# Products of ones on TensorE ahead of the first transposes of k, q and P

## The chip, the cores and the metric

The kernel runs on one core of one Trainium2 chip. The metric is the time of one execution in microseconds (us). Three executions of the kernel before took 773.11, 776.22 and 777.68 us, a median of 776.22 us. One more execution was profiled; all durations below come from that one.

## The reference

Two layers, one after the other. Attention with pooled queries: q, k and v are (4, 8, 1152, 64) in float32; pairs of query rows are averaged, so that 576 query rows per head meet 1152 keys. Then a feed-forward layer over the 2304 tokens of 512 features, with a squared ReLU between two matrices of 512 x 2048 and 2048 x 512.

```
q_pool = q.reshape(B, H, S // 2, 2, D).mean(axis=3)
scores = (1 / sqrt(D)) * q_pool @ k.T
attn   = exp(scores - max(scores)); attn = attn / (sum(attn) + 1e-09)
x      = (attn @ v), heads laid side by side: (2304, 512)
out    = relu(x @ w_in) ** 2 @ w_out
```

## The kernel before

**Tiling.** Two heads of one batch are a pair; there are 16 pairs. A pair's 2 x 576 query rows are cut into 9 chunks of 128 rows, so there are 144 chunks, each with a score tile of 128 x 1152. For a chunk TensorE forms the scores (S), VectorE finds the row maximum (MX), ScalarE takes the exponential and its row sum (EX), giving P. P is then transposed, and multiplied by v (PV). Once a block of 256 tokens has all its heads it goes through the feed-forward layer: H (first matrix, line 1033), the square, O (second matrix, line 1082). There are nine such blocks.

**Precision.** In most pairs operands are split into a high and a low 16-bit part, and transposed by DMA. The first pair takes another way (`full_s`): its k and q are transposed on TensorE in float32, as products with the identity, into PSUM banks "ba", and copied from there: KX (k, three groups of 6 matmuls, line 423) with its copies KC (lines 415 and 417), QS (the sum of query pairs on VectorE, line 400), QY (q, two groups, line 436) with its copies QC. The scores of this pair are float32 too (line 653, two chunks at a time). The chunks of the first four pairs (`full_v`) transpose their P on TensorE in float32: TP (line 750, three groups of 3 matmuls) with copies TC (lines 760 and 762). A float32 matmul has two records in the trace, one matmul in the program.

**Beside it.** While the first chunks run, the weights are loaded in 16 pieces of 1 MB (line 1136) and converted: 1144, 1150 and 1163 are ScalarE's steps of a piece, 1153, 1169 and 1178 VectorE's (some of them go to GpSimd). Line 466 is a product of the raw k, q or v with itself (GR), which gives that pair's scale; line 470 takes its maximum (GM).

**What sets the order.** A table, `ORDER`, lists every step with its engine and its buffer. Each engine runs its steps strictly in that order, and waits by semaphores for what it reads and for buffers that others must give back. There are two banks "ba" until the last chunk is done; the six banks "bt" come later. The DMAs are issued from SP's queue, in order as well: the load of the second pair's k (line 369) waits until KX has read the first pair's, the load of the second q (line 377) until QY has.

The functions `kx`, `qy` and `tp4` are emitted for KX, QY and TP; `bank(o, ...)` gives the bank that the table chose for the step. `ones` is a column of 128 ones in bfloat16, written by the first instruction of VectorE (line 1326).

Of the kernel before, what the change touches and what calls it, by code (L numbers as in the profile page):

```python
# [16 lines left out]
AX = mybir.AxisListType  # L17
PSUM = bass.MemoryType.PSUM

CFG = {'SPLIT': 0, 'TURN': [], 'TURNB': [], 'WDP': ((1, 0), (1, 1), (1, 2), (1, 3)), 'WSP': 0.4394, 'WOF': 23.2581, 'MSP': 10.7319, 'FV': (0, 1, 2, 3), 'PART': 1, 'QXD': (1, 2, 3, 4), 'MSC': (0, 1, 2, 3, 4, 5, 6, 7, 8, 9, 10, 11, 12, 13, 14, 15), 'FS': (0,), 'NSG': (12, 13, 14, 15)}  # L20


def cfg(k, d):
    return CFG.get(k, d)

# [73 lines left out]
class Plan:  # L99
# [7 lines left out]
    def add(self, name, engs, deps, emit, at, take=None, give=None, after=()):  # L107

        self.at[name] = len(self.ops)
        self.ops.append(  # L110
            dict(name=name, engs=engs, deps=[d for d in deps if d], emit=emit, take=take, give=give, after=after)
        )
# [30 lines left out]
def kernel(  # L143
# [12 lines left out]
    nc = tc.nc  # L156
# [27 lines left out]
    ones = c_p.tile([128, 1], BF16, name="ones")  # L184
# [56 lines left out]
    def bank(o, *shape):  # L241
        r, x = plan.slot[o["name"]]
        t = banks[r][x]
        if not shape:
            return t
        return t[:, : shape[0] * shape[1]].rearrange("p (a b) -> p a b", a=shape[0])

    def buf(*key):
        r, x = plan.slot[key]
        return bufs[r][x]  # L250
# [12 lines left out]
    def alt(kind, **engs):  # L263
        on = cfg("alt", {}).get(kind, ALT.get(kind, ""))
        return {e: c for i, (e, c) in enumerate(engs.items()) if i == 0 or e[0] in on}
# [25 lines left out]
    def kT(n):  # L291
        s = preps[n]["slot"]
        return kTs[s] if s is not None else buf("kT", n).rearrange("p (a b) -> p a b", b=128)

    def qT(n):
        s = preps[n]["slot"]
        return qTs[s] if s is not None else buf("qT", n).rearrange("p (l c m) -> p l c m", l=2, c=9)

    def k4(n):
        return kT(n).rearrange("p a b -> p (a b)").bitcast(F32).rearrange("p (c k) -> p c k", c=9)  # L300

    def q4(t):
        return t.rearrange("p l c m -> p (l c m)").bitcast(F32).rearrange("p (c m) -> p c m", m=64)
# [13 lines left out]
    def pslot(vi, j, full):  # L317
        t = PT.rearrange("p a s b -> p (a s b)")
        if full:
            t = t.bitcast(F32)  # L320
        a = pcol(vi, j)
        return t.rearrange("p (a x) -> p a x", x=896)[:, :, a : a + 128]
# [24 lines left out]
    def prep(n):  # L347
# [11 lines left out]
        def rk():  # L359
            return raw("k", n).rearrange("p (h c d) -> p h c d", h=2, c=9)  # L360
# [4 lines left out]
        def rq():  # L365
            return raw("q", n).rearrange("p (c r d) -> p c r d", c=9, r=2)
# [35 lines left out]
        def k2():  # L402
            return buf("k2", n).rearrange("p (h c l d) -> p h c l d", h=2, c=9, l=2)
# [5 lines left out]
        if n in full_s:  # L409
            assert not keep  # L410
            kt4, qt4 = k4(n), q4(qT(n))

            def move(o, out, x):
                if o["eng"] == "ACT":
                    nc.scalar.activation(out, x, AF.Copy)
                else:
                    nc.vector.tensor_copy(out, x)

            def kx(o, x):
                tl["kx", n, x] = t = bank(o, 3, 128)  # L420
                for y in range(3):
                    for h in range(2):
                        nc.tensor.matmul(
                            t[h * 64 : h * 64 + 64, y], lhsT=rk()[:, h, 3 * x + y, :], rhs=ident,
                            start=True, stop=True, skip_group_check=True,
                        )

            def kc(o, x):
                move(o, kt4[:, 3 * x : 3 * x + 3], tl.pop(("kx", n, x)))

            def qy(o, z):
                tl["qy", n, z] = t = bank(o, 5, 64)
                for y in range(5 - z):
                    for h in range(2):
                        hs = slice(h * 64, h * 64 + 64)
                        nc.tensor.matmul(t[hs, y], lhsT=rq()[:, 5 * z + y, 0, :], rhs=ident[:, h : h + 127 : 2], start=True, stop=True, skip_group_check=True)

            def qc(o, z):
                t = tl.pop(("qy", n, z))
                if z == 0:  # L440
                    move(o, qt4[:, :5], t)
                else:
                    move(o, qt4[:, 5:8], t[:, :3])
                    for h in range(2):
                        hs = slice(h * 64, h * 64 + 64)
                        move(o, qt4[hs, 9 + h], t[hs, 3])

            add(("QS", n), qse, [("LQ", n)], qsum, need)
            for x in range(3):
                add(("KX", n, x), {"PE": 1270}, [("LK", n) + ((x,) if n == 0 and x < 2 else ())] + old, lambda o, x=x: kx(o, x), need, take=(("KX", n, x), ("a",), 0), give=("k", n) if x == 2 else None)  # L450
                add(("KC", n, x), alt("KC", ACT=380, DVE=460), [("KX", n, x)] + old, lambda o, x=x: kc(o, x), need, give=("KX", n, x))
            for z in range(2):
                add(("QY", n, z), {"PE": 760 - 150 * z}, [("QS", n)] + old, lambda o, z=z: qy(o, z), need, take=(("QY", n, z), ("a",), 0), give=("q", n) if z else None)
                add(("QC", n, z), alt("QC", ACT=350 + 350 * z, DVE=400 + 300 * z), [("QY", n, z)] + old, lambda o, z=z: qc(o, z), need, give=("QY", n, z))
# [170 lines left out]
    def chunk(i):  # L625
# [71 lines left out]
        def P():  # L697
            return buf("P", i).bitcast(F32)
# [44 lines left out]
        if n in full_v:  # L743
            pt = pslot(vi, j, True)

            def tp4(o, x):
                t = bank(o, 3, 128)
                for y in range(3):
                    c = 3 * x + y
                    nc.tensor.matmul(  # L750
                        t[:, y], lhsT=P()[:, c * 128 : (c + 1) * 128], rhs=ident, is_transpose=True,
                        start=(y == 0), stop=(y == 2), skip_group_check=True,
                    )
                tl["tp", i, x] = t

            def tc4(o, x):
                t = tl.pop(("tp", i, x))
                out = pt[:, 3 * x : 3 * x + 3]
                if o["eng"] == "ACT":
                    nc.scalar.activation(out, t, AF.Copy)  # L760
                else:
                    nc.vector.tensor_copy(out, t)

            for x in range(3):
                add(("TP", i, x), {"PE": 400}, [("EX", i)] + ring + ([("TP", i, x - 1)] if x else []), lambda o, x=x: tp4(o, x), i, take=(("TP", i, x), ("a",), 0), give=("P", i) if x == 2 else None)
                add(("TC", i, x), alt("TC", ACT=380, DVE=460), [("TP", i, x)] + ring, lambda o, x=x: tc4(o, x), i, give=("TP", i, x))
            return
# [603 lines left out]
```

## Time and profile before

| | |
|---|---|
| median of three runs | 776.22 us (773.11 to 777.68) |
| profiled execution | 777.25 us |
| its span, first to last instruction | 775.5 us |
| TensorE busy | 736.0 us, 95% of the span |
| VectorE busy | 580.1 us, 75% |
| ScalarE busy | 525.5 us, 68% |
| GpSimd busy | 318.0 us, 41% |
| mean granted clock of TensorE | 0.997 |

The profiled execution's own time is 1.75 us longer than its span, for what lies around the first and last instruction. "Granted clock" (PEclk) is the share of TensorE's full clock that its throttle let through: 1.00 is 2.4 GHz, 0.50 is 1.2 GHz. A row of the timeline gives the start, the duration, the engine, the line, the operation, what it writes and reads, and in square brackets how long the engine had idled and who released it.

### The profile page before, as it was taken

To read this page: it belongs to the slowest core of one execution; us is meant where nothing else is said; L and a number is where in the kernel's file an instruction comes from. 1 tells how busy PE (TensorE), PEld (TensorE's weight loads), DVE (VectorE), ACT (ScalarE), POOL (GpSimd) and SP (SyncE) were. 2 spreads that over 40 slices of the span, in tenths; PEclk is the share of its full clock that TensorE was granted. 3 is DMA by queue.
4 is the path that set the end of the run, shared out by engine and by line. 5 is a ranking of instruction groups with operands and counts; after the bars stand their busy time and mean duration, and the time that the engine had idled before them with its cause. 6 is when DMAs were issued, how large, how long until landed. Compare 5 with 4: busy or idle time off the path is not lost. (4 is left out here: it accounts for less than half of the span.)

```text
span 775.5 us, 15240 instructions
## 1 busy us (share of the span) xinstructions
PE 736.0 (95%) x5998; PEld 485.5 (63%) x5998; DVE 580.1 (75%) x983; ACT 525.5 (68%) x830; POOL 318.0 (41%) x221
## 2 busy tenths in 40 slices
PE   5889899999999999998999999999999999999997
PEld 4555556557756765567655865685577558576763
DVE  2998998899987878789988998889778872414032
ACT  3989978889885786678876787785698542323030
POOL 0434422356445464483262355536665431122001
PEclk9999999999999999999999999999999999999999
DMA  7694782519999999999999999999999946001011
GB/s 284 230 283 136 231 232 86 123 41 225 195 216 193 208 209 214 194 216 189 221 214 213 197 220 216 191 214 200 200 205 172 193 82 119 1 1 28 2 29 27
DMA packets 324840, 128.96 MB, mean 166 GB/s; under 512 B 307104, under 2 KB 307872, under 8 KB 324768
## 3 DMA queue, kind: packets, MB, share of 16 engines
q1 hardware_dynamic: 324768, 127.98, 79.8%
q8 instruction: 47, 0.77, 0.4%
q14 instruction: 25, 0.20, 0.1%
HBM read 45.09 MB, written 4.72 MB: 64 GB/s over the span
## 5 line engine op out<-in xcount | busy, mean ns | idle before, releaser
L685 DVE TENSOR_SCALAR_CACHE_REDUCE s<-s,esc 128x1152 f32<-128x1152 f32 x135 | 190.6, 1421 | 27.2 <-PE s L674 23.4
L709 ACT ACTIVATE buf<-s,ca 128x1152 f32<-128x1152 f32 x144 | 175.1, 1217 | 44.0 <-POOL ca L695 13.4
L1033 PEld LDWEIGHTS <-w 128*128 128x128 f16 x1728 | 167.3, 98 | 27.4 <-issue 4.7
L721 POOL TENSOR_TENSOR buf<-buf,buf 128x1152 f16<-128x1152 f32 x49 | 121.4, 2479 | 83.3 <-ACT buf L713 49.1
L1082 PE MATMUL ba<-w,region 128*128 128x512 f16 x672 | 152.9, 379 | 0.3 <-ACT ru L931 0.3
L1082 PEld LDWEIGHTS <-region 128*128 128x128 f16 x864 | 82.7, 98 | 95.6 <-issue 1.8
L674 PE MATMUL s<-kT,qT 128*128 128x512 f16 x720 | 134.3, 326 | 6.1 <-ACT buf L709 4.2
L1033 PE MATMUL ba<-region,w 128*128 128x256 f16 x1056 | 121.2, 273 | 2.5 <-DVE psc L515 1.0
L674 PEld LDWEIGHTS <-qT 128*128 128x128 f16 x720 | 63.3, 99 | 62.1 <-issue 11.9
L1060 POOL TENSOR_TENSOR region<-region 128x512 f16<-128x512 f32 x37 | 47.5, 1286 | 121.1 <-DVE region L1056 74.6
L721 DVE TENSOR_TENSOR buf<-buf,buf 128x1152 f16<-128x1152 f32 x59 | 84.8, 1442 | 7.1 <-POOL buf L282 2.4
L869 PE MATMUL ba<-PT,v 128*64 128x320 f16 (+1 forms) x1296 | 84.4, 287 | 0.3 <-DMA PT<-buf 0.3
L869 PEld LDWEIGHTS <-v 128*64 128x64 f16 x1296 | 70.9, 110 | 13.2 <-issue 5.7
L713 ACT ACTIVATE buf<-buf 128x1152 f16<-128x1152 f32 x62 | 71.6, 1156 | 8.4 <-DMA PT<-buf 3.3
L1048 ACT ACTIVATE region<-region 128x512 f16<-128x512 f32 x72 | 44.0, 622 | 32.4 <-DVE region L1045 32.1
L750 PE MATMUL ba<-ident,buf 128*128 128x128 f32 x324 | 52.9, 287 | 12.7 <-ACT PT L760 5.8
L1033 PE MATMUL bt<-region,w 128*128 128x256 f16 x480 | 53.9, 273 | 0.0
L750 PEld LDWEIGHTS ba<-ident,buf 128*128 128x128 f32 x324 | 34.1, 141 | 29.1 <-ACT PT L760 11.2
L282 POOL TENSOR_SCALAR buf<-buf,cols 128x1152 f16<-128x1152 f32 x24 | 34.1, 1422 | 30.4 <-ACT buf L709 24.4
L1082 PE MATMUL bt<-w,region 128*128 128x512 f16 x192 | 43.6, 379 | 0.0
L760 ACT ACTIVATE PT<-ba 128x384 f32<-128x384 f32 x81 | 37.1, 490 | 9.3 <-PE ba L750 8.9
L1043 ACT ACTIVATE region<-bt 128x512 f32<-128x512 f32 x11 | 6.4, 593 | 49.1 <-PE bt L1033 26.4
(191 smaller groups left out, 928.2 us busy)
## 6 DMA issues: line engine op xcount, KB each, us to landing
raw<-in_q_dram SPq DMA_DIRECT2D x32, 288.0 KB, 4.0
raw<-in_k_dram SPq DMA_DIRECT2D x15, 576.0 KB, 5.2
region<-in_moe_w_in_dram SPq DMA_DIRECT2D x8, 1024.0 KB, 5.4
w<-in_moe_w_out_dram SPq DMA_DIRECT2D x8, 1024.0 KB, 6.1
raw<-in_v_dram SPq DMA_DIRECT2D x12, 576.0 KB, 4.6
v<-in_v_dram SPq DMA_DIRECT2D x4, 576.0 KB, 6.6
out_dram<-half SPq DMA_DIRECT2D x18, 128.0 KB, 2.5
out_dram<-buf SPq DMA_DIRECT2D x18, 128.0 KB, 2.4
```

The source lines that it names most:

```text
L674: nc.tensor.matmul(s[:, x, :w], lhsT=qt[:, l].rearrange("p c m -> p (c m)")[:, 128 * c0 + h : 128 * c0 + h + 255 : 2], rhs=rhs, **st)
L685: nc.vector.tensor_scalar(st3(), st3(), sc, 3e38, op0=ALU.mult, op1=ALU.min, accum_out=a[:, x : x + 1])
L709: nc.scalar.activation(P(), st3(), AF.Exp, bias=a[:, 1:2], scale=s1, accum_out=col)
L713: nc.scalar.activation(hl()[:, 0], P(), AF.Copy)
L721: e.tensor_tensor(out=hl()[:, 1], in0=P(), in1=hl()[:, 0], op=ALU.subtract)
L750: nc.tensor.matmul(t[:, y], lhsT=P()[:, c * 128 : (c + 1) * 128], rhs=ident, is_transpose=True, start=(y == 0), stop=(y == 2), skip_group_ ...
L760: nc.scalar.activation(out, t, AF.Copy)
L869: nc.tensor.matmul(px[h * 64 : (h + 1) * 64, 64 * r * (1 - h) : 64 * r * (1 - h) + N], lhsT=vv[:, h, kc, vl, :], rhs=p2(vi, r, h, 9 * pl + ...
L1033: nc.tensor.matmul(ph[:, f2], lhsT=w16[0][:, SLOT[f // 4], wl, a, f % 4 * 128 : (f % 4 + 1) * 128], rhs=xhl()[:, xl, a], start=(i == 0), s ...
L1048: nc.scalar.activation(gt[u][:, 0], rt[u % 2], AF.Square)
L1060: e.tensor_tensor(out=gt[u][:, 1], in0=rt[u % 2], in1=gt[u][:, 0], op=ALU.subtract)
L1082: nc.tensor.matmul(p[:, :DM], lhsT=g[:, gl, f % 2, tt * 128 : (tt + 1) * 128], rhs=w16[1][:, SLOT[f // 4], wl, f % 4], start=(f == 0 and g ...
```

## The change

A function `busy` is added, and called as the first thing in `qy`, `kx` and `tp4`, once the bank is chosen. A new entry `BUSY` of the table of settings says for which steps it does something: 7 products before KX 0 of the first pair, 14 before its QY 0, 10 before TP 0 of chunk 0. A product is a 128 x 128 matrix of ones times a 128 x 512 matrix of ones, both read from the one column, in bfloat16, into the bank that the following transposes fill; these overwrite it, and nobody reads it. The order of all steps, their engines and their buffers stay.

```
-CFG = {'SPLIT': 0, ...
+CFG = {'BUSY': {('KX', 0, 0): 7, ('QY', 0, 0): 14, ('TP', 0, 0): 10}, 'SPLIT': 0, ...
...
+    def busy(o):
+
+        for _ in range(cfg("BUSY", {}).get(o["name"], 0)):
+            nc.tensor.matmul(bank(o), lhsT=ones.to_broadcast([128, 128]), rhs=ones.to_broadcast([128, 512]), start=True, stop=True)
...
             def kx(o, x):
                 tl["kx", n, x] = t = bank(o, 3, 128)
+                busy(o)
...
             def qy(o, z):
                 tl["qy", n, z] = t = bank(o, 5, 64)
+                busy(o)
...
             def tp4(o, x):
                 t = bank(o, 3, 128)
+                busy(o)
```

In the listings that follow a row is a line, an operation, what it writes and reads, the shape, and the semaphores that it waits for: DMAHW are DMA queues, Pool is GpSimd, Activation is ScalarE. raw_101 is the first pair's k, raw_102 its q, ba_114 and ba_115 the two banks. Line numbers of the changed kernel are 6 to 8 higher from `kx` on.

TensorE before, from the program's start to the first transposes of q:

```order
L423 MATMUL ba_114<-ident,raw_101 64x128 [waits DMAHW0_49,Pool_49]
L423 MATMUL ba_114<-ident,raw_101 64x128 x5
L423 MATMUL ba_115<-ident,raw_101 64x128 [waits DMAHW1_49]
...
L423 MATMUL ba_114<-ident,raw_101 64x128 [waits DMAHW2_49,DVE_49]
...
L436 MATMUL ba_115<-ident,raw_102 64x64 [waits DMAHW3_49,DMAHW4_49,DVE_49,Activation_49]
```

TensorE of the changed kernel, the same place:

```order
L251 LDWEIGHTS ones [waits DVE_49]
L251 MATMUL ba_114<-ones 128x512
...
L429 MATMUL ba_114<-ident,raw_101 64x128 [waits DMAHW0_49,Pool_49]
...
L429 MATMUL ba_115<-ident,raw_101 64x128 [waits DMAHW1_49]
...
L429 MATMUL ba_114<-ident,raw_101 64x128 [waits DMAHW2_49,DVE_49]
...
L251 MATMUL ba_115<-ones 128x512 [waits Activation_49]
...
L443 MATMUL ba_115<-ident,raw_102 64x64 [waits DMAHW4_49,DMAHW3_49,DVE_49]
```

Seven products stand first, which wait only for VectorE's `ones`. Fourteen stand between the transposes of k and of q; the first of them takes over the wait for ScalarE's copy out of ba_115, and the wait for q and its sum stays with the first transpose.

TensorE before, from the product of the second k with itself to the first transposes of P (buf_93):

```order
L466 LDWEIGHTS raw_101 [waits DMAHW6_49]
L466 MATMUL ba_115<-raw_101 128x128
...
L750 MATMUL ba_114<-ident,buf_93 128x128 [waits Activation_49]
```

The changed kernel there:

```order
L473 LDWEIGHTS raw_101 [waits DMAHW6_49]
L473 MATMUL ba_115<-raw_101 128x128
...
L251 LDWEIGHTS ones
L251 MATMUL ba_114<-ones 128x512 [waits Activation_49]
...
L758 MATMUL ba_114<-ident,buf_93 128x128 [waits Activation_49]
```

Ten products stand behind the product of k; they wait for ScalarE's earlier copy out of ba_114, and the transposes for ScalarE's P. On the four other queues the instructions and their waits stand as before.

## Rows read from the trace of the kernel before

**Rows 1.** Busy time by stage: us, busy and count of each engine, PEclk, DMA share, GB/s.
```profile
0.00:16.00 16.00, 9.93 (x82) 7.42 (x84) 2.45 (x10) 5.84 (x9) 0.99 (x8) 1.00 0.82 292
16.00:19.50 3.50, 1.26 (x17) 0.97 (x14) 3.10 (x6) 1.85 (x4) 0.00 (x0) 1.00 0.61 242
19.50:23.00 3.50, 3.50 (x12) 2.03 (x12) 3.34 (x5) 3.50 (x6) 0.00 (x0) 0.51 0.34 87
23.00:40.00 17.00, 13.22 (x104) 8.92 (x101) 16.87 (x25) 15.28 (x23) 9.42 (x5) 1.00 0.77 270
...
130.00:500.00 370.00, 356.67 (x3010) 234.25 (x3006) 321.80 (x568) 292.79 (x456) 182.09 (x117) 1.00 1.00 192
```

**Rows 2.** Timeline of TensorE, the first 26 us.
```profile
3.51 4.11 PE L423 MATMUL ba<-ident,raw 128*64 128x128 f32 x36 [3.51 <-DMA raw<-in_k_dram]
10.17 2.19 PE L436 MATMUL ba<-ident,raw 128*64 128x64 f32 x36 [2.56 <-DVE raw L400]
12.29 4.08 PE L653 MATMUL s<-kT,qT 64*128 64x512 f32 x12
16.30 0.69 PE L466 MATMUL ba<-raw 128*128 128x128 bf16 x9
19.23 1.31 PE L750 MATMUL ba<-ident,buf 128*128 128x128 f32 x6 [2.24 <-ACT buf L709]
20.47 3.44 PE L653 MATMUL s<-kT,qT 64*128 64x512 f32 x12
23.84 0.88 PE L750 MATMUL ba<-ident,buf 128*128 128x128 f32 x6
25.43 0.68 PE L466 MATMUL ba<-raw 128*128 128x128 bf16 x9 [0.71 <-ACT PT L760]
```

**Rows 3.** Timeline of TensorE from 36 to 46 us: the same kinds later.
```profile
37.01 2.21 PE L653 MATMUL s<-kT,qT 64*128 64x512 f32 x12
...
41.15 4.11 PE L861 MATMUL ba<-PT,v 128*64 128x256 f32 x36 [0.58 <-ACT PT L760]
```

**Rows 4.** Chain of work that ended last (start, us, what), and the shape of its line.
```profile
767.84 2.60 PE ba L1082 x12
```
```profile
L1082 PE MATMUL ba<-w,region 128*128 128x512 f16 x672 | 152.9, 379 | 0.3 <-ACT ru L931 0.3
```

**Rows 5.** Timeline of VectorE, the first 25 us.
```profile
0.81 0.06 DVE L1326 MEMSET ones<- 128x1 bf16 x1 [0.81 <-PEq L1355]
...
5.09 0.56 DVE L417 COPY kT<-ba 128x384 f32<-128x384 f32 x1 [3.22 <-PE ba L423]
9.31 0.76 DVE L400 TENSOR_TENSOR raw<-raw 128x576 f32<-128x576 f32 x1 [3.66 <-DMA raw<-in_q_dram]
11.61 0.49 DVE L417 COPY qT<-ba 128x320 f32<-128x320 f32 x1 [1.54 <-PE ba L436]
16.40 1.37 DVE L685 TENSOR_SCALAR_CACHE_REDUCE s<-s 128x1152 f32<-128x1152 f32 x1 [4.30 <-PE s L653]
...
22.79 1.22 DVE L1169 SCALAR_TENSOR_TENSOR w<-w,region 128x1024 int32<-128x1024 int32 x1
23.92 1.36 DVE L685 TENSOR_SCALAR_CACHE_REDUCE s<-s 128x1152 f32<-128x1152 f32 x1
```

**Rows 6.** Timeline of ScalarE from 11 to 25 us.
```profile
12.40 0.66 ACT L415 ACTIVATE qT<-ba 128x192 f32<-128x192 f32 x3 [4.26 <-PE ba L436]
13.07 1.13 ACT L1144 ACTIVATE w<-region 128x1024 f32<-128x1024 f32 x1
...
15.10 1.12 ACT L1163 ACTIVATE region<-region 128x1024 int32<-128x1024 uint16 x1
17.86 1.22 ACT L709 ACTIVATE buf<-s,ca 128x1152 f32<-128x1152 f32 x1 [1.65 <-DVE s L685]
...
21.41 1.14 ACT L1163 ACTIVATE region<-region 128x1024 int32<-128x1024 uint16 x1
```

**Rows 7.** Waits of VectorE, 0 to 47 us: total us, times, longest.
```profile
DVE s L685 <- PE s L653: 4.3, 1, 4.3
...
DVE w L1169 <- ACT w L1144: 0.5, 1, 0.5
...
DVE PT L762 <- PE ba L750: 0.2, 1, 0.2
```

**Rows 8.** SP's queue, 0 to 13 us.
```profile
3.53 0.59 SPq L1136 DMA_DIRECT2D region<-in_moe_w_in_dram  x1
7.64 0.37 SPq L369 DMA_DIRECT2D raw<-in_k_dram  x1
```

**Rows 9.** DMA issues of these two moments: KB each, us to landing.
```profile
region<-in_moe_w_in_dram SPq DMA_DIRECT2D x1, 1024.0 KB, 8.2
```
```profile
raw<-in_k_dram SPq DMA_DIRECT2D x1, 576.0 KB, 5.7
```

**Rows 10.** Busy time by stage, 40 to 60 us, columns as in the first group.
```profile
40.00:46.80 6.80, 6.22 (x52) 3.71 (x51) 6.34 (x9) 6.13 (x9) 2.14 (x1) 1.00 1.08 311
46.80:60.00 13.20, 10.93 (x92) 7.42 (x90) 11.74 (x15) 11.21 (x21) 4.40 (x3) 1.00 1.07 262
```

More of the change, by code (lines that the diff above doesn't have):

```diff
@@ L18 @@
 PSUM = bass.MemoryType.PSUM
-CFG = {'SPLIT': 0, 'TURN': [], 'TURNB': [], 'WDP': ((1, 0), (1, 1), (1, 2), (1, 3)), 'WSP': 0.4394, 'WOF': 23.2581, 'MSP': 10.7319, 'FV': (0, 1, 2, 3), 'PART': 1, 'QXD': (1, 2, 3, 4), 'MSC': (0, 1, 2, 3, 4, 5, 6, 7, 8, 9, 10, 11, 12, 13, 14, 15), 'FS': (0,), 'NSG': (12, 13, 14, 15)}
+CFG = {'BUSY': {('KX', 0, 0): 7, ('QY', 0, 0): 14, ('TP', 0, 0): 10}, 'SPLIT': 0, 'TURN': [], 'TURNB': [], 'WDP': ((1, 0), (1, 1), (1, 2), (1, 3)), 'WSP': 0.4394, 'WOF': 23.2581, 'MSP': 10.7319, 'FV': (0, 1, 2, 3), 'PART': 1, 'QXD': (1, 2, 3, 4), 'MSC': (0, 1, 2, 3, 4, 5, 6, 7, 8, 9, 10, 11, 12, 13, 14, 15), 'FS': (0,), 'NSG': (12, 13, 14, 15)}
 def cfg(k, d):
@@ L246, in bank, with busy @@
         return t[:, : shape[0] * shape[1]].rearrange("p (a b) -> p a b", a=shape[0])
+    def busy(o):
+        for _ in range(cfg("BUSY", {}).get(o["name"], 0)):
+            nc.tensor.matmul(bank(o), lhsT=ones.to_broadcast([128, 128]), rhs=ones.to_broadcast([128, 512]), start=True, stop=True)
     def buf(*key):
@@ L420, in kx @@
                 tl["kx", n, x] = t = bank(o, 3, 128)
+                busy(o)
                 for y in range(3):
@@ L432, in qy @@
                 tl["qy", n, z] = t = bank(o, 5, 64)
+                busy(o)
                 for y in range(5 - z):
@@ L747, in tp4 @@
                 t = bank(o, 3, 128)
+                busy(o)
                 for y in range(3):
```

## The prediction

> **What bounds the kernel now.** I read the busy time by stage first, then TensorE's timeline of the first 24 us, then VectorE's and ScalarE's timelines and VectorE's waits there, and SP's queue last. From 130 to 500 us TensorE is busy 356.67 of 370 us [rows 1]: the long middle hangs on TensorE's order, and nothing of it is touched. The change lies in the first 24 us, and what it is worth is the time by which everything behind them starts earlier. Who holds the work up there? VectorE begins the first row maximum at 16.40, after 4.30 us of idling for the scores of line 653 [rows 5], and from there to 47 us it waits for no more than 0.2 and 0.5 us [rows 7]; from 23 to 40 us it is busy 16.87 of 17 us [rows 1]. So the start is a chain on TensorE (transposes of k, of q, first scores), and from 16.40 on VectorE, with ScalarE close beside it, is the bound.
>
> TensorE runs that first chain slowly. The score pass of two chunks takes 4.08 us at 12.29 and 2.21 us at 37.01, with the same 12 records [rows 2, 3]. The 36 records of line 423 take 4.11 us for 128 columns; line 861's 36 take the same 4.11 us for 256 columns [rows 2, 3]. Both are a factor of two: the start runs at half clock, 1.2 GHz. The product of k with itself at 16.30, 9 in 0.69 us as at 25.43 (0.68), is the first work at full speed, after TensorE had worked without a gap from 10.17. Then it idles 2.24 us; the granted clock is 0.51 from 19.50 to 23.00 [rows 1], and the second score pass takes 3.44 us.
>
> The column of the granted clock prints 1.00 for the first 16 us [rows 1], which the durations contradict. The Trainium skill (TensorE: Matmul & The Clock Gate, "What's actually happening") says that the throttled state is the default and that activity releases it; the durations agree with it, the column doesn't. By the column there would be nothing to win and the sum would be 0; by the rule and the durations it is the one below.
>
> **The change part by part.** It removes nothing, adds 31 products, and moves no step. One product is a 16-bit matmul of 128 x 512; twelve of that shape take 2.60 us back to back with their weight loads [rows 4], 0.217 us each, and so 0.434 us at half clock.
>
> *Seven before k.* They wait for `ones`, written at 0.81 to 0.87 [rows 5]; with a first weight load I put the first product at 1.05. Seven at half clock take 3.04 us and end at 4.1. Line 423 began at 3.51 [rows 2], so k's transposes start 0.6 us later. What follows depends on when the clock rises. No row shows what products of ones do to it. The nearest rows are the two rises: in the one TensorE had worked since 10.17 and was fast at 16.30, in the other since 19.23 and was fast at about 22.9 to 23 (6.1 and 3.7 us) [rows 1, 2]. Taken from 1.05, the rise would come between 4.7 and 7.2. The transposes need 4.11 us at half clock, half of that at full: begun at 4.1, they end at 6.5 with the early rise and 7.7 with the late one, against 7.62 before. The bank of the third group comes free with VectorE's copy of 0.56 us [rows 5], which fits in. So the 0.6 us are hidden or nearly so.
>
> *Fourteen before q.* At full clock 3.04 us: they end at 9.5 (early) to 10.7 (late). The sum of q is ready when line 436 starts, at 10.17 [rows 2], after q's landing and VectorE's 0.76 us [rows 5]; the products can't move that. So q's transposes start between 10.17 and 10.7, and cost 1.1 instead of 2.19 us. The score pass then needs the copy of the first 20 of 36 records: 0.61 us of transposes, a copy of 0.49 us [rows 5] and some 0.15 us between them, 1.25 us in all, so it starts at 11.4 to 11.95 instead of 12.29.
>
> *The first scores.* 2.21 us [rows 3] instead of 4.08: they end at 13.65 to 14.2 against 16.37. Of that the row maximum makes 2.2 to 2.7 us.
>
> *ScalarE.* The first exponential began at 17.86, 1.46 us behind the start of its row maximum [rows 5, 6]: 15.1 to 15.7 now. But ScalarE has other work in front: the last copy of q, 0.67 us, and three weight steps until 16.22 [rows 6]. It now starts these when q's transposes end (11.3 to 11.8); the weights they read are issued at 3.53 and land 8.2 us later, 11.7 [rows 8, 9], so no wait is added, and the exponential can begin at 15.2 to 15.7. It gains 2.15 to 2.65 us, 2.4 in the middle. The second k is issued behind line 423 and lands 5.7 us after 7.64, at 13.3 [rows 8, 9]; its product follows the scores at 13.65 or later, so no wait arises there.
>
> *Ten before P.* The k product ends 0.7 us behind the scores, at 14.35 to 14.9; ten products take 2.17 us and end at 16.5 to 17.1. P is there 1.22 us after the exponential began (1.37 us from 17.86 to 19.23 before [rows 2, 6]): 16.6 to 17.1. They fit without delay, and the gap that preceded the second slow stretch is filled. The stretch's own price is 0.43 us for the transposes (1.31 against 0.88 [rows 2]) and 1.23 us for the second score pass (3.44 against 2.21 [rows 2, 3]), 1.66 together. I count it as nothing: that pass ends at 23.91, and VectorE comes to it at 23.92 straight from line 1169, which began at 22.79, behind ScalarE's line 1163 that ended at 22.55 [rows 2, 5, 6]. With the spell gone VectorE and ScalarE are late by themselves.
>
> *Behind 24 us.* The later loads wait for steps of VectorE and TensorE and move with these. So 2.4 us is carried through: 777.25 - 2.4 = 774.85 against the profiled execution's own time. That execution lies 1.03 us above the median of the three runs, from which the same step gives 773.8. I predict 774.3, between the two.
>
> **The rivals.**
>
> *The second slow stretch is on the path as well.* VectorE and the score pass meet within 0.01 us at 23.9; should ScalarE's and VectorE's steps there close up more than I think, the 1.66 us come on top: 4.06 us, 773.2 or, from the median, 772.2. Against it stands that VectorE has no wait between 16.40 and 24 but one of 0.2 us [rows 7].
>
> *The gain is lost to the loads.* From 40 to 60 us the DMA engines are loaded 1.07 to 1.08 by their own share [rows 10]; if that stretch runs at the pace of the transfers, an earlier start is waited away there, and the time is 776.2 to 777.2. Against it: the DMA share is only 0.34 from 19.5 to 23 [rows 1], so they too can start earlier.
>
> *The clock rises late.* If the transposes of k don't help to raise the clock, k ends at 8.2, and the fourteen products raise it somewhere between their middle and their end. If at the end, they take 6.08 us to 14.3, q's transposes follow, the scores start at 15.5 and end at 17.7: 1.3 us later than before. If in the middle (11.2), the other seven end at 12.8, the scores start at 14.0 and end at 16.2: 0.15 us earlier. The time would be 777.1 to 778.6. For it speaks that k's 4.11 us were followed by slow transposes of q, though with 2.56 us of idling between [rows 2]. The Trainium skill (the same page, "Part 4: PE-mode transpose") says that transposes don't count as a busy TensorE in the same way, and sides with this rival; the trace has no rise that only transposes preceded.
>
> *The products don't raise it at all*, and stay in the way. k ends at 8.2, the fourteen at 14.3, q at 16.5, the first scores after 4.08 us at 20.55 against 16.37: 4.2 us late, 781.4 or more. It turns into a loss that can be told once the fourteen and the scores behind them both run at half clock. Against it: plain matmuls did raise the clock twice [rows 1, 2].
>
> **How the numbers follow.** The forecast of 2.15 to 2.65 us gets 0.56; the second stretch on the path 0.14; lost to the loads 0.15; the late rise 0.10; no rise 0.05. Half a per cent, 3.9 us, is about what a measurement of this kernel can tell from no change (the three runs lie 4.6 us apart): below 772.3 is faster, above 780.1 slower. The second rival's price lies at that border and the forecast 2 us from it, so with the runs' scatter I give faster 0.22; no rise and some scatter give slower 0.07; the rest, 0.71, is the same. The range, 771.5 to 778.0, takes in the forecast, the first rival, the loads and half of the late rise.
>
> **What the profile would show.** Products from about 1.05 at 0.43 us each, and 0.22 us each ahead of q; q's transposes at 10.2 to 10.7 in 1.1 us; the first score pass in 2.2 us, ending at 13.7 to 14.2; no slow stretch at 19.5; the first exponential at 15.2 to 15.7, right behind line 1163's steps; and the same 2.4 us at the row maximum that began at 23.92. The prediction is wrong if the first row maximum moves by under 1.5 us, or if it moves by 2.4 and the end doesn't.

## The result, and the profile after

The changed kernel is slower: 779.59 us (776.37 to 784.54, 16 runs) against 774.76 us (772.21 to 778.76, 16 runs), a ratio of 1.0067 (95% interval 1.0049 to 1.0085). By the ratio that is 5.2 us (the medians lie 4.8 apart), where a gain of about 2 was forecast. The profiled execution took 779.02 us with a span of 777.2 us.

The start did what the steps said. TensorE's timeline of the changed kernel (start, length, engine, line, operation, count, and in brackets the idle time before and who ended it):

```profile
0.93 3.17 PE L251 MATMUL ba<-ones 128*128 128x512 bf16 x7 [0.93 <-DVE ones L1334]
4.03 2.90 PE L429 MATMUL ba<-ident,raw 128*64 128x128 f32 x36
6.86 3.23 PE L251 MATMUL ba<-ones 128*128 128x512 bf16 x14
...
10.03 1.27 PE L443 MATMUL ba<-ident,raw 128*64 128x64 f32 x36
11.49 2.21 PE L660 MATMUL s<-kT,qT 64*128 64x512 f32 x12 [0.20 <-DVE qT L422]
13.64 0.69 PE L473 MATMUL ba<-raw 128*128 128x128 bf16 x9
14.17 2.35 PE L251 MATMUL ba<-ones 128*128 128x512 bf16 x10
16.56 0.87 PE L758 MATMUL ba<-ident,buf 128*128 128x128 f32 x6
17.36 2.71 PE L660 MATMUL s<-kT,qT 64*128 64x512 f32 x12
```

Seven products take 3.17 us, and the fourteen behind them 3.23, so TensorE goes from 1.2 to 2.4 GHz within k's transposes, which take 2.90 us where they took 4.11 [rows 2]. The first scores take 2.21 instead of 4.08 us. The other two engines follow; their timelines in the same kernel:

```profile
7.61 0.76 DVE L405 TENSOR_TENSOR raw<-raw 128x576 f32<-128x576 f32 x1 [1.61 <-DMA raw<-in_q_dram]
13.73 1.37 DVE L692 TENSOR_SCALAR_CACHE_REDUCE s<-s 128x1152 f32<-128x1152 f32 x1 [2.29 <-PE s L660]
21.10 1.36 DVE L692 TENSOR_SCALAR_CACHE_REDUCE s<-s 128x1152 f32<-128x1152 f32 x1
...
97.78 1.42 DVE L692 TENSOR_SCALAR_CACHE_REDUCE s<-s,esc 128x1152 f32<-128x1152 f32 x1
...
15.19 1.22 ACT L716 ACTIVATE buf<-s,ca 128x1152 f32<-128x1152 f32 x1
```

The first row maximum starts 2.67 us earlier (13.73 against 16.40 [rows 5]), the first exponential 2.67 (15.19 against 17.86 [rows 6]), the row maximum of 23.92 now at 21.10, 2.82 earlier. The row maximum at 97.78 is one that starts at 101.43 in the profile of before (shown with hold below), so near 100 us the lead is still there, 3.65 us. By stage (length, busy time and count of TensorE, its weight loads, VectorE, ScalarE and GpSimd, then clock, DMA share and GB/s):

```profile
16.00:19.50 3.50, 3.46 (x19) 2.05 (x18) 3.50 (x7) 3.50 (x6) 0.00 (x0) 1.00 0.79 271
19.50:23.00 3.50, 1.62 (x15) 1.11 (x13) 3.50 (x5) 3.50 (x7) 1.73 (x1) 1.00 0.88 298
...
130.00:500.00 370.00, 353.92 (x2981) 231.60 (x2980) 319.00 (x563) 290.62 (x452) 178.96 (x116) 1.00 1.01 192
```

The clock of 0.51 between 19.50 and 23.00 [rows 1] is gone. But from 130 to 500 us TensorE is busy 353.92 instead of 356.67 us, with 29 fewer instructions done: the middle, which the change doesn't touch, has more idling. It comes in single waits. Two of them, which end at 108.2 and 472.7 us in the changed kernel, from its list of TensorE's waits (total us, times, longest):

```profile
PE s L681 <- DMA kT<-buf: 1.8, 1, 1.8
...
PE s L681 <- DMA kT<-buf: 1.5, 1, 1.5
```

Scores wait for a transpose of k that the DMA engines do. A second run of the kernel before, looked at below, waits 0.4 us at the first place and not at all at the second. So there are two questions: why is the gain of 2.7 us not there at the end, and what makes these transposes late?

### The profile page after: what moved, and what is told of

The parts are those of the page before. It is cut to its first block, busy times and chain, and to the rows that moved or that the text cites. A ratio compares the mean times of both kernels' runs of the same rounds, so it can differ in the third digit from the quotient of the medians.

```text
span 777.2 us, 15301 instructions
## 1 busy us (share of the span) xinstructions
PE 739.6 (95%) x6029; PEld 484.7 (62%) x6029; DVE 583.5 (75%) x983; ACT 525.0 (68%) x830; POOL 314.5 (40%) x221
## 5 line engine op out<-in xcount | busy, mean ns | idle before, releaser
L728 DVE TENSOR_TENSOR buf<-buf,buf 128x1152 f16<-128x1152 f32 x59 | 83.1, 1412 | 7.9 <-POOL buf L287 3.1
L877 PEld LDWEIGHTS <-v 128*64 128x64 f16 x1296 | 70.8, 110 | 15.7 <-issue 6.0
```

The lines of the kernel that those rows point to most:

```text
L728: e.tensor_tensor(out=hl()[:, 1], in0=P(), in1=hl()[:, 0], op=ALU.subtract)
L877: nc.tensor.matmul(px[h * 64 : (h + 1) * 64, 64 * r * (1 - h) : 64 * r * (1 - h) + N], lhsT=vv[:, h, kc, vl, :], rhs=p2(vi, r, h, 9 * pl + ...
```

## The experiments

Theory A: the 62 instructions (each product is a weight load and a matmul) move every later load of TensorE's own instructions by 62 places, and some then fall into transposes of k or q for which TensorE waits. Theory B: the earlier start itself puts the later loads and steps into a worse order. Theory C, added when the first results were in: the early gain is measured against an execution in which q came late. All expectations were written before their runs.

**pad62**: 62 instructions ahead of k, which take 0.99 us in an idle stretch; k's transposes behind them take 4.11 us as before.

```
                 tl["kx", n, x] = t = bank(o, 3, 128)
+                for _ in range(31 if (n, x) == (0, 0) else 0):
+                    nc.tensor.matmul(bank(o)[:32, :16], lhsT=ones.to_broadcast([128, 32]), rhs=ones.to_broadcast([128, 16]), start=True, stop=True)
```

> The kernel before with 31 tiny products (32 x 128 by 128 x 16) in front of the first transposes of k, where TensorE idles until 3.5 us anyway: as many added instructions of TensorE as the change has (62), but next to no work, so that the start does not move. Theory A (the change costs by where TensorE's own instruction loads fall: 62 instructions more in front move each of the 16 KB loads, so that other DMA transposes meet one): slower than before by about 5 to 7 us, 780 to 782 us. Theory B (the change costs by the earlier start: work and transfers meet at other moments): no change, 774 to 776 us, since nothing starts earlier.

**after256**: the change with 128 smaller products, 256 instructions, for about the same time of TensorE.

```
-CFG = {'BUSY': {('KX', 0, 0): 7, ('QY', 0, 0): 14, ('TP', 0, 0): 10}, 'SPLIT': 0, ...
+CFG = {'BUSY': {('KX', 0, 0): 29, ('QY', 0, 0): 58, ('TP', 0, 0): 41}, 'SPLIT': 0, ...
...
-            nc.tensor.matmul(bank(o), lhsT=ones.to_broadcast([128, 128]), rhs=ones.to_broadcast([128, 512]), start=True, stop=True)
+            nc.tensor.matmul(bank(o)[:64, :124], lhsT=ones.to_broadcast([128, 64]), rhs=ones.to_broadcast([128, 124]), start=True, stop=True)
```

> The changed kernel with its 31 products of 512 columns cut into 128 products of 124 columns (weights of 64 columns), 29, 58 and 41 at the three places: the same time on TensorE within some tenths of a us, but 256 added instructions instead of 62, which is one whole 16 KB load. The loads of TensorE's instructions then stand at the same work as in the kernel before. Theory A: the loss goes and the early gain stays, 771 to 773 us. Theory B: as the changed kernel, 779 to 780 us.

**hold**: the change, with two copies on VectorE that put its first row maximum back to where it was.

```
+            for _ in range(2 if i == 0 else 0):
+                nc.vector.tensor_copy(PT.rearrange("p a s b -> p (a s b)").bitcast(F32)[:, :1152], st3())
```

> The changed kernel with two extra copies of the first score tile on VectorE (1152 columns each, about 2.6 us together) ahead of the first row maximum: the early start is taken back, and from the first row maximum on everything should stand at the times of the kernel before, with the 62 added instructions of TensorE in place. Theory A: slower than the changed kernel or equal to it, 780 to 783 us. Theory B: as the kernel before, 774 to 776 us.

| kernel | us | ratio to the kernel before |
|---|---|---|
| pad62 | 779.33 (776.86 to 781.39) | 1.0079 (1.0059 to 1.0100) |
| after256 | 774.53 (772.35 to 779.41) | 1.0030 (1.0011 to 1.0049) |
| hold | 782.45 (782.01 to 782.65) | 1.0119 (1.0097 to 1.0141) |

The kernel before took 773.04 us beside them. pad62 has no long products and loses as much as the change; hold stands at the times of before at 16 and at 101 us and loses still. VectorE's timeline of hold, and behind it that row maximum in before:

```profile
16.33 1.36 DVE L694 TENSOR_SCALAR_CACHE_REDUCE s<-s 128x1152 f32<-128x1152 f32 x1
...
101.55 1.42 DVE L694 TENSOR_SCALAR_CACHE_REDUCE s<-s,esc 128x1152 f32<-128x1152 f32 x1
```

```profile
101.43 1.42 DVE L685 TENSOR_SCALAR_CACHE_REDUCE s<-s,esc 128x1152 f32<-128x1152 f32 x1
```

Hold is 0.12 us behind there, and 5.1 us behind near the end, at the block of 96 matmuls shown below (646.06 against 640.93). So the loss needs neither an early start nor long products, and theory B falls with that. after256 lost much less than the change, which speaks for A, but not nothing.

**pad128** and **pad256**: as pad62, with 64 tiny products ahead of k, and with 72 ahead of k and 56 ahead of P (in `tp4`). **noq256**: 256 instructions by `busy`, which now takes two counts, with 12 products of 124 columns and 48 tiny ones ahead of k, only 20 tiny ones ahead of q, 28 and 20 ahead of P. **again**: the kernel before, unchanged, for a second profile. The first two lines show pad128 against pad62; the last is a summary.

```
-            for _ in range(31 if (n, x) == (0, 0) else 0):
+            for _ in range(64 if (n, x) == (0, 0) else 0):      (pad128; 72 in pad256)
...
+                for _ in range(56 if (i, x) == (0, 0) else 0):  (pad256, in tp4, the same tiny matmul)
...
+BUSY (wide, tiny): KX (12, 48), QY (0, 20), TP (28, 20)         (noq256)
```

> The kernel before with 64 tiny products (32 x 128 by 128 x 16) in front of the first transposes of k: 128 added instructions of TensorE, half of one 16 KB load, some 2 us of idle time filled. Theory A (where the loads of TensorE's instructions fall decides): another place, so another time than the kernel before, in a direction that it can't tell; 770 to 782 us, and not the 779 of 62 added instructions unless by chance. Rival (added instructions cost by their number): twice the loss of 62 of them, about 785 us.

> The kernel before with 128 tiny products, 72 in front of the first transposes of k and 56 in front of the first transposes of P, where TensorE idles: 256 added instructions, one whole 16 KB load. Theory A: the later loads stand at the same work as in the kernel before, so its time again, 772 to 775 us. Rival (their number): four times the loss of 62, over 790 us. Rival (any change of the start loses because the order was tuned to this one): 777 to 781 us.

> 256 added instructions, but no long products in front of the transposes of q: 12 products of 124 columns and 48 tiny ones ahead of k, 20 tiny ones (0.6 us) ahead of q, 28 of 124 columns and 20 tiny ones ahead of P. Theory C (in most executions q lands earlier than in the profile of the kernel before, so that the fourteen products hold up q's transposes, and the early gain is small or none): faster than the version with 58 products of 124 columns ahead of q, by up to 1.5 us, 772 to 774 us. If q mostly lands as late as in that profile: no difference to it, 774 to 775 us.

> The kernel before, unchanged, profiled once more. Theory C: the sum of q starts near 7.6 us as in the profiles of the three other kernels, not at 9.31, and the first row maximum 2 to 4 us earlier than 16.40. Otherwise both stand where they stood.

| kernel | us | ratio to the kernel before |
|---|---|---|
| pad128 | 774.76 (772.65 to 779.50) | 1.0006 (0.9978 to 1.0035) |
| pad256 | 775.62 (772.34 to 780.56) | 1.0017 (0.9988 to 1.0045) |
| noq256 | 776.77 (772.93 to 780.05) | 1.0023 (0.9997 to 1.0049) |
| again | 774.28, one execution | |

The kernel before took 774.71 us. Twice and four times as many instructions ahead cost nothing that can be told: it is not their number. Nor is an early start enough for a loss: the first row maximum starts at 12.03 in pad128 and at 11.76 in pad256, and at 12.23 in pad62, which loses. noq256 missed: it was to beat after256. Its profile shows one reason; its TensorE timeline:

```profile
14.02 0.69 PE L476 MATMUL ba<-raw 128*128 128x128 bf16 x9 [1.81 <-DMA raw<-in_k_dram]
14.64 2.96 PE L252 MATMUL ba<-ones 128*64 128x124 bf16 x28
17.53 0.70 PE L254 MATMUL ba<-ones 128*32 128x16 bf16 x20
18.16 0.89 PE L761 MATMUL ba<-ident,buf 128*128 128x128 f32 x6
```

Its first row maximum was early, at 12.24, but then the product of k waited 1.81 us for the second k, and the products ahead of P, which are in order behind it, held P's transposes until 18.16, later than the 16.56 of the changed kernel.

The profile of again settles theory C. Rows of TensorE, VectorE and ScalarE in that second execution of the kernel before:

```profile
8.72 2.19 PE L436 MATMUL ba<-ident,raw 128*64 128x64 f32 x36 [0.71 <-DVE raw L400]
10.85 2.72 PE L653 MATMUL s<-kT,qT 64*128 64x512 f32 x12
7.87 0.76 DVE L400 TENSOR_TENSOR raw<-raw 128x576 f32<-128x576 f32 x1 [2.23 <-DMA raw<-in_q_dram]
13.60 1.37 DVE L685 TENSOR_SCALAR_CACHE_REDUCE s<-s 128x1152 f32<-128x1152 f32 x1 [2.94 <-PE s L653]
15.06 1.22 ACT L709 ACTIVATE buf<-s,ca 128x1152 f32<-128x1152 f32 x1 [0.28 <-DVE s L685]
```

The sum of q starts at 7.87 here, at 9.31 in the profile of before [rows 5], and between 6.93 and 8.08 in all ten other profiles. With q in time the kernel before reaches its first exponential at 15.06, the changed one at 15.19. The early gain against such an execution is nil: the fourteen products hold q's transposes until 10.03, though q's sum was done at 8.4, and what the faster clock gives back behind them only makes up for it. The clock of 1.00 between 19.50 and 23.00 is not the products' doing alone: again shows it too.

A third profile with the start unchanged is that of late62, whose edit (below) stands at 678 us. Its TensorE and VectorE:

```profile
3.47 3.65 PE L423 MATMUL ba<-ident,raw 128*64 128x128 f32 x36 [3.47 <-DMA raw<-in_k_dram]
8.00 1.28 PE L436 MATMUL ba<-ident,raw 128*64 128x64 f32 x36 [0.88 <-DVE raw L400]
11.70 1.37 DVE L685 TENSOR_SCALAR_CACHE_REDUCE s<-s 128x1152 f32<-128x1152 f32 x1 [2.29 <-PE s L653]
```

Here the clock rose within k's transposes with nothing ahead of them on TensorE (3.65 us, against 4.11 in before and 2.90 behind the products), and the first row maximum starts at 11.70, 2.0 us earlier than in the changed kernel. The unchanged start spreads from 11.70 to 16.40, and the forecast took the slowest of three as its base.

**pad208** and **pad176**: 104 and 88 tiny products ahead of k. Theory A was put to work here: moved by how many instructions would the loads meet the fewest transposes of k and q? **late62**: 62 instructions too, but at the start of the last part, behind all transposes.

```
+            for _ in range(104 if (n, x) == (0, 0) else 0):      (pad208; 88 in pad176)
...
+                for _ in range(31 if (j, u) == (border[-2], 0) else 0):   (late62, in h, the same tiny matmul)
```

> The kernel before with 104 tiny products (208 instructions) in front of the first transposes of k, about 3 us, half a us of it behind the landing of k. In the second profile of the kernel before I moved its 47 loads of TensorE's instructions back by so many instructions and counted the DMA transposes of k and q that would have one between issue and landing: 12 with none added, 19 with 64, 13 with 128, 12 with 176, 9 or 7 with 176 to 208, 10 with 256. Theory A with this count: 208 is the best place, faster than the kernel before by 2 to 4 us, 770.5 to 773 us. Rival (added instructions can only lose): 775 us or more.

> The kernel before with 88 tiny products (176 instructions) in front of the first transposes of k. By the same count 9 transposes of k and q meet a load, against 12 in the kernel before. Theory A: faster by 1 to 3 us, 771.5 to 774 us, and 5 us or more below the version with 62. Rival (added instructions can only lose): 775 us or more.

> The kernel before with 31 tiny products (62 instructions) ahead of the first group of line 1033 of the last block but one, after the attention's work: TensorE runs without a gap there, so they cost their own time, about 1 us. Theory A (62 instructions cost because they move the later loads among the transposes): no more than this 1 us, 775 to 776.5 us, since no transpose is behind them. Rival (62 instructions cost wherever they stand): 780 us.

(In the text for pad208 the counts for 176 and 208 are garbled; the text for pad176 gives 9 for 176.)

| kernel | us | ratio to the kernel before |
|---|---|---|
| pad208 | 775.10 (768.43 to 778.56) | 1.0007 (0.9981 to 1.0033) |
| pad176 | 777.88 (770.82 to 781.61) | 1.0026 (0.9994 to 1.0057) |
| late62 | 774.19 (772.29 to 782.84) | 1.0019 (0.9990 to 1.0049) |

The kernel before took 775.00 us. late62 came as expected, with no loss that can be told; its TensorE timeline shows the price of 31 tiny products, 0.93 us:

```profile
678.06 0.93 PE L1029 MATMUL bt<-ones 128*32 128x16 bf16 x31
```

pad208 and pad176 were to be faster by 1 to 4 us and weren't: the forecast count of meetings doesn't rank kernels.

What the profiles tell apart is the changed places of the loads. The DMA views of the transpose of k issued at 102.6 in again, and at 100.7 in the changed kernel, each from its issue to its landing (queue: packets, MB, share; then the issue's line, KB where known, and us to landing), again first:

```profile
q1 hardware_dynamic: 2703, 1.68, 110.7%
...
kT<-buf SPq DMA_TRANSPOSE x1, 6.1
```

```profile
q1 hardware_dynamic: 2853, 2.23, 106.3%
q8 instruction: 1, 0.02, 0.8%
...
kT<-buf SPq DMA_TRANSPOSE x1, 7.5
```

The changed kernel has one load of instructions in it and takes 1.4 us longer. The same transpose in hold and in pad62:

```profile
q8 instruction: 1, 0.02, 0.7%
...
kT<-buf SPq DMA_TRANSPOSE x1, 7.5
```

```profile
q8 instruction: 1, 0.02, 0.8%
...
kT<-buf SPq DMA_TRANSPOSE x1, 7.6
```

and in late62, where 62 instructions are added behind it:

```profile
q1 hardware_dynamic: 2720, 1.75, 111.8%
...
kT<-buf SPq DMA_TRANSPOSE x1, 6.0
```

In the packed trace a landing has sixteen parts. In again they come 5.89 to 6.09 us behind the issue. In the changed kernel fifteen come at 5.78 to 5.95, and one at 7.47, with the load starting at 5.46; hold shows the same, and in pad62 all sixteen come at 7.46 to 7.64. TensorE waits for this landing 0.4 us in again and late62, 1.8 in the changed kernel and hold, 2.1 in pad62.

It isn't the only place. The transpose of k that again issues at 464.8, and the changed kernel at 466.1, in the same view:

```profile
kT<-buf SPq DMA_TRANSPOSE x1, 4.9
```

```profile
q8 instruction: 1, 0.02, 0.9%
...
kT<-buf SPq DMA_TRANSPOSE x1, 6.5
```

hold and pad62 took 6.7 and 6.6 us there, before and late62 4.9 and 4.8. Here the DMA view shows what the engines do around the load. GB/s moved from 469 to 474 us, in slices of 0.125 us, in the changed kernel and in again:

```profile
GB/s 227 221 215 207 213 225 195 123 168 168 248 232 238 268 135 70 10 0 0 0 0 8 8 10 10 10 10 233 293 287 293 289 293 291 287 289 291 293 289 208
```

```profile
GB/s 238 240 227 209 209 201 209 219 215 215 217 199 203 334 231 106 12 0 0 0 2 6 8 10 10 10 8 195 291 295 287 726 221 369 590 0 590 590 37 479
```

In both a load starts at 470.7, and from 471.0 to 472.4 next to nothing is moved. In the changed kernel k's transpose is under way, and the scores wait for it. In again that one landed at 469.6; it is a transpose of P (467.6, landing 5.9 us later) that pays, and TensorE doesn't wait for it.

This holds in every kernel. Of the 138 steps that transpose k, q or P by DMA, 128 meet a load in some of the twelve profiles and none in others (a load counts that starts behind the issue, and 0.3 us or more before the shortest landing of that step). With a load they land 0.9 us later on the mean, and later in 121 of the 128. The number of meetings tells the kernels apart badly: between 90 and 600 us a load starts between issue and landing of a transpose of q or k 14, 16 and 12 times in the changed kernel, hold and pad62, and 6 to 11 times in the nine others; counted 1 to 6 us behind the issue, it is 12 or 13 times against 7 to 13. Nor do the loads differ much in number: 47, or 48 where 176 instructions or more were added. What differs is where they fall.

And it adds up to about the loss. From the row maximum that starts at 101.43 in before to the start of the block of 96 matmuls near the end (line 1033 there), so without the start of the kernel:

| instructions ahead | us from one to the other |
|---|---|
| 0 (again, before, late62) | 538.3, 539.5, 538.2 |
| 256 (after256, pad256, noq256) | 539.3, 538.5, 540.3 |
| 128, 208, 176 | 541.0, 541.1, 543.0 |
| 62 (after, hold, pad62) | 544.9, 544.5, 545.9 |

The ends of it, in the TensorE timelines of again, the changed kernel and hold:

```profile
637.96 10.64 PE L1033 MATMUL bt<-region,w 128*128 128x256 f16 x96
```

```profile
642.72 10.64 PE L1041 MATMUL bt<-region,w 128*128 128x256 f16 x96
```

```profile
646.06 10.64 PE L1043 MATMUL bt<-region,w 128*128 128x256 f16 x96
```

With 62 ahead this stretch is 4.2 to 7.7 us longer than with 0 or 256, about what the change loses. Each number is one execution, and executions of one kernel lie up to 10 us apart; those of noq256 and pad176 were 2.6 and 2.7 us above their kernel's median, so 540.3 and 543.0 may be high. In the stretch TensorE idles 21.1, 18.3 and 19.7 us in the changed kernel, hold and pad62, and 14 to 17 in the nine others. A good part is its waits for k's transposes, again first, then the changed kernel, hold and pad62 (0.2 to 1.8 us in the other eight):

```profile
PE s L674 <- DMA kT<-buf: 0.4, 1, 0.4
```

```profile
PE s L681 <- DMA kT<-buf: 3.4, 2, 1.8
```

```profile
PE s L681 <- DMA kT<-buf: 3.0, 2, 1.8
```

```profile
PE s L676 <- DMA kT<-buf: 3.5, 2, 2.1
```

Most of the rest are waits for VectorE, 6.9 to 7.9 us against 2.4 to 5.3 in the nine others; that VectorE is late for the same reason is not shown. The clock doesn't explain the changed kernel: from 100 to 640 us its mean granted clock in every stage of 100 us is 1.00, as in again. It explains a part of the two others: hold and pad62 have two such stages at 0.98 each, and TensorE is busy 526.2 us in their stretch, against 523.8 in the changed kernel and 522.8 in again. 256 instructions are about one load's worth: TensorE's records lie 255 apart from load to load on the mean (the trace lacks some records). In the three kernels with 256 ahead, as in again, no load falls into the two transposes of k above. The Trainium skill (Runtime: NRT & Kernel Launch, "Instruction fetch mechanics") says that an engine's instructions are fetched in blocks of 16 KiB, 256 instructions, over a DMA queue of the engine's own. The trace agrees: 47 or 48 loads of 16,384 bytes in this queue. The Trainium skill calls the cost of such a boundary mostly hidden; here no wait of TensorE between 98 and 643 us in the changed kernel is put down to its own instructions, but the transposes that the loads meet come later.

What stays open: which meetings count. pad176 and pad208 have the fewest (6 and 7) and yet longer stretches than 0 or 256; their transpose of k at 104.2 and 101.6 took 9.2 and 9.1 us without a load in it, while the transpose of q before it met one. Why the DMA engines stop when both meet isn't shown either, and no kernel without the loads was run.

## Why the prediction was wrong, step by step

- *Clock, products, transposes, scores*: right, in part by luck. The clock rises within k's transposes; the products take 3.17, 3.23 and 2.35 us (3.04, 3.04, 2.17 forecast), the scores end at 13.7 and the exponential starts at 15.19 (15.2 to 15.7). But q's transposes started at 10.03 because the products ended there, not because q was ready, so these times agree by chance. The two rivals in which the clock rises late or not at all are out: k's transposes took 2.90 instead of 4.11 us. The Trainium skill (TensorE: Matmul & The Clock Gate, "Part 4: PE-mode transpose"), which the prediction put on the side of the late rise, speaks of TensorE's transpose mode; k's transposes here are plain products with the identity, and in late62 the clock rose with nothing but them ahead of it (3.65 us).
- *The second slow stretch*: it went, and was worth nothing, as forecast: 2.67 us of gain at the first row maximum, 2.82 at the one behind it. That is 0.15 us more, not 1.66: the rival that put it on the path is out. Without any products it is missing in again (the second scores take 2.71 us) and there in late62 (4.27).
- *"The sum of q is ready when line 436 starts, at 10.17"*: this failed. The fourteen products were priced as hidden behind q's late arrival, which is the property of one execution; q's sum is ready by 7.7 to 8.8 in the eleven others. Against again the start gains nothing (13.73 against 13.60 at the first row maximum), against late62 it loses 2.0 us, and this takes the whole 2.4 us from the sum. That the profiled execution lay 1.03 us above the median was seen and spread evenly; it should have been looked for in the row that the sum hung on. Over 16 runs the kernel before came to 774.76 us, so the forecast of 774.3 was nearly that of no change.
- *"Moves no step", "2.4 us is carried through"*: this failed too. The lead was carried as far as 97.78 us and lost behind it. A term is missing: 62 instructions more on TensorE move its instruction loads, worth 4 to 8 us here (544.5 to 545.9 against 538.2 to 540.3 us). Without it and with the corrected start the sum would be no change. The kernels with 256 instructions come near that, 1.0017 to 1.0030; the 0.3% of after256 (1.0011 to 1.0049) is clear of none, and its cause is open.
- *The rival "lost to the loads"* had the right kind of place, the DMA engines at full load, and the wrong stretch and cause: from 40 to 60 us nothing was lost (the lead is 2.82 us at 21 and 3.65 at 98), and after 100 us it is not an earlier start that is waited away, since hold starts as late as before and loses more.
- The prediction named its own sign of failure: the row maximum moves by 2.4 us and the end doesn't. That is what came, in the profiles.

## What to carry to other kernels

Before a sum hangs on when one transfer lands, read that landing in a second profile of the same kernel: a spread of 2 us in one load was the whole of this gain. Instructions added to a full engine need not be free though they run in idle time: they shift all later instruction loads, and in a kernel whose DMA engines are full and feed TensorE with transposes just in time, this cost 0.7 to 1.2% with 62 instructions, and nothing that can be told with 128. To judge an edit of that size, compare it with a copy in which as many instructions without effect stand in the same place, or fill it up to 256 (here 1.0017 to 1.0030).

## What the runs showed of the hardware that was not expected

A load of 16 KB, 0.02 MB among 2.23 in the same window, stands beside a transpose that lands 1.4 to 1.8 us later (6.1 to 7.5, 4.9 to 6.7), and around it the DMA engines move next to nothing for 1.4 us (471.0 to 472.4). Over all steps the mean is 0.9 us. 62 instructions of no use ahead of all work changed the time of a 775 us kernel by 0.8% (pad62, 1.0059 to 1.0100), without any change in the order of its steps. And q's landing, with the same queue ahead of it, moved its sum between 6.93 and 9.31 us from one execution to the next.
